# The order of units around the last attention pair, and the leftover tile of a mixture layer

## The chip, the cores and the metric

The kernel runs on one core of a Trainium2 chip. Its engines have their own instruction queues and meet through semaphores: PE (matrix products), DVE (vector), ACT (activations and copies), POOL (casts, and DMAs that convert types or use indices) and SP (which here only issues DMAs). The metric is the device time of one execution in microseconds (us), as the median over runs. Lower is better.

## The reference

Attention with one shared key and value head, then a mixture of 16 experts in 4 groups, one expert per token:

```
scores = scale * np.matmul(q, k.transpose(0, 1, 3, 2))      # q (8, 16, 384, 64), k and v (8, 1, 384, 64)
attn = softmax(scores);  out = np.matmul(attn, v)
x = out as (8 * 384, 16 * 64)                               # 3072 tokens of 1024
g = argmax(x @ w_group)                                     # 4 groups, with weight g_w (softmax)
e = argmax(x @ w_expert[g])                                 # 4 experts of the group, with weight e_w
out[token] = g_w * e_w * (relu(x[token] @ w1[g, e]) @ w2[g, e])
```

In the data that is drawn, nearly all tokens of a batch item choose one expert. The kernel makes use of that, and computes what is left over by itself.

## The kernel before

**Attention.** It works in 24 pairs p of a batch item b (8) and a third st of its 384 tokens. For each pair `scores` (L251) makes six blocks of 64 keys on PE, ACT takes exponentials (L253), DVE sums them over blocks (`pre_add`, L259 and L261) and folds the sum over keys (`fold_keys`, L265). `values` (L290) multiplies the exponentials with v, six blocks into one PSUM tile `o`. `join` (L273) adds the folded sums on PE, `invert` (L278, L280) inverts and spreads them, and `weigh` multiplies `o` by them (L300) to xT, the token rows transposed; POOL casts them to xbf (L301), and after an item's third pair SP writes xbf to DRAM (L303, x_bf). The loop over p runs the scores of pair p beside the values of pair p - 1. The values of the last pair have no scores beside them; they come behind the loop, L611 to L615.

**Gates and weights.** `gates` (L312) makes an item's gate logits on PE, `counts` (L338, L340) counts on PE how many tokens chose each expert, ACT copies the counts from PSUM (L342), and DVE picks the most frequent expert from the first third (`choose_b`). POOL's queue then loads that expert's weights, w1 in four DMAs of 512 KB (L145) and w2 in one of 2 MB (L357), casting f32 to bf16. Weight tiles have two buffers. `gate_c` (L386 to L395) makes each token's weight for the chosen expert, gsel, and marks further pairs of item and expert that any token chose.

**Units.** The chosen expert is computed for the item's 384 tokens in 14 units, which `fill(n)` takes from a list: 8 h units (L407: eight matmuls of 384 columns; ACT ReLU L408 into hT) and 6 y units (L415: eight matmuls of 512 columns; ACT scales them by gsel, L416, into a row tile y, which SP stores when both halves are there, L436). h0 to h7 and y0 to y5 below are an item's units. `fill` follows the 24 pairs in bursts (`PHASES`): the 8 h units of item 6 are the last burst in the loop, after pair 22, with the gates of item 7 after three of them, the counts after five and `early_pair` after six. Its y units come two at a time behind the loop.

**The leftover tile.** `early_pair` (L511) picks the one (item, expert) pair that is expected to be left over, as an index into 128 pairs; `fill` starts loading its w1 after item 6's last h unit and its w2 (L547) after item 6's last y unit. Behind the loop the kernel counts and ranks that pair's tokens: a prefix product on PE (L642, L643, `pr`), a selection matrix of up to 32 tokens, `pick`, in four copies (L653), and their weights and output rows (L659, `pg`; `gc`, `rows`). The item's tokens are read back from x_bf (L626, `xe`), which waits for the write of L303. They are transposed on PE (L681, `pb`), gathered by `pick` (L692, `px`), multiplied by w1 (L700, `ph`), transposed (L705, `phT`) and multiplied by w2 (L712, `py`), with copies on DVE and ACT between. Quarters of the columns lie in four groups of 32 partitions. POOL scatters the result into `out` by rows (L715), which replaces what the y units stored there, and so waits for the earlier stores of `out`. In the kernel before all item 7's units stand ahead of `px`. Then a flag in a register of each engine (`rare`) decides whether a general path runs; with this data it does not.

Order on each engine is as written: PE, DVE, ACT, POOL and SP run their instructions in the order in which the program names them. PSUM tiles named by `side` share three buffers, so each waits until the one three places back was read.

Of the kernel before, what the change touches and what calls it, by code (L numbers as in the profile page):

```python
# [9 lines left out]
FP32 = mybir.dt.float32  # L10
# [3 lines left out]
P = 128  # L14
ACTF = mybir.ActivationFunctionType
# [6 lines left out]
def kernel(  # L22
# [372 lines left out]
        nc.vector.reduce_sum(out=gs[:], in_=gm[:], axis=AX)  # L395
        gsel[b] = gs

    def moe_units(w1, w2, xb, gs_of, place, store):
        units = []
        state = {}  # L400

        def h_unit(fc):
            if fc == 0:
                state["h"] = pool.tile([P, FO, S], BF16, tag="hT", bufs=1, name="hT")
            ps = side([P, CW], FP32, "hps")
            for ko in range(KO):
                nc.tensor.matmul(out=ps[:, 0:S], lhsT=w1[:, ko, fc * P:(fc + 1) * P], rhs=xb[:, ko, :], start=(ko == 0), stop=(ko == KO - 1))  # L407
            nc.scalar.activation(out=state["h"][:, fc, :], in_=ps[:, 0:S], func=ACTF.Relu)  # L408

        def y_unit(st, nh):  # L410
            cs = slice(nh * CW, (nh + 1) * CW)
            y = place(st, cs)
            ps = side([P, CW], FP32, "yps")
            for fo in range(FO):
                nc.tensor.matmul(out=ps[:], lhsT=state["h"][:, fo, st * P:(st + 1) * P], rhs=w2[:, fo, nh * CW:(nh + 1) * CW], start=(fo == 0), stop=(fo == FO - 1))  # L415
            nc.scalar.activation(out=y, in_=ps[:], func=ACTF.Copy, scale=gs_of()[:, st:st + 1])  # L416
            store(st, cs, y)

        for fc in range(FO):
            units.append(lambda fc=fc: h_unit(fc))  # L420
        for st in range(ST):
            for nh in range(2):
                units.append(lambda st=st, nh=nh: y_unit(st, nh))
        return units

    def first_units(b):
        rows = {}

        def place(st, cs):
            if cs.start == 0:  # L430
                rows[st] = pool.tile([P, Dm], FP32, tag="y", bufs=3, name="y")
            return rows[st][:, cs]

        def store(st, cs, y):
            if cs.stop == Dm:
                nc.sync.dma_start(out=outv[b, :, st, :], in_=rows[st][:])  # L436
        return moe_units(wts[b][0], wts[b][1], xbf[b], lambda: gsel[b], place, store)

    NP = B * ST

# [70 lines left out]
    def early_pair():  # L511
        last = B - 1
        mask = pool.tile([P, GE], FP32, tag="mask", bufs=1, name="mask1")
        idf = pool.tile([P, 1], FP32, tag="idf", bufs=1, name="idf1")
        nc.vector.tensor_copy(out=idf[:], in_=choice[last][:, 0:1])
        nc.vector.tensor_scalar(out=mask[:], in0=iota16[:], scalar1=idf[:, 0:1], scalar2=None, op0=OP.is_equal)
        nc.vector.scalar_tensor_tensor(out=extra[:, last * GE:NPAIR], in0=seen[last], scalar=0.0, in1=mask[:], op0=OP.is_gt, op1=OP.subtract)
        known = pool.tile([P, 1], FP32, tag="known", bufs=1, name="known")
        nc.vector.reduce_sum(out=known[:], in_=extra[:], axis=AX)
        top = pool.tile([P, 8], FP32, tag="top", bufs=1, name="top2")  # L520
        idx = pool.tile([P, 8], U32, tag="idx2", bufs=1, name="idx2")
        nc.vector.max_with_indices(out_max=top[:], out_indices=idx[:], in_=extra[:])
        pf = pool.tile([P, 1], FP32, tag="pf", bufs=1, name="pf")
        nc.vector.tensor_copy(out=pf[:], in_=idx[:, 0:1])
        base = pool.tile([P, 1], U32, tag="base", bufs=1, name="base")
        nc.vector.tensor_scalar(out=base[:], in0=idx[:, 0:1], scalar1=NPAIR - GE, scalar2=None, op0=OP.bitwise_and)
        basef = pool.tile([P, 1], FP32, tag="basef", bufs=1, name="basef")
        nc.vector.tensor_scalar(out=basef[:], in0=base[:], scalar1=float(S // GE), scalar2=None, op0=OP.mult)
        gi = pool.tile([P, ST, 2], FP32, tag="gi", bufs=1, name="gi")
        nc.vector.tensor_scalar(out=gi[:, :, 1], in0=tokid[:], scalar1=basef[:, 0:1], scalar2=None, op0=OP.add)  # L530
        reg = nc.values_load(idx[0:1, 0:1], engines=(ET.Pool, ET.DVE, ET.SP), min_val=0, max_val=NPAIR - 1, skip_runtime_bounds_check_because="an index into 128 flags")
        leftover.update(known=known, pf=pf, gi=gi, reg=reg)

    def parts_of(pair):
        e_reg = nc.s_assert_within(pair & (GE - 1), 0, GE - 1, skip_runtime_bounds_check_because="the bits of an index below 128")
# [13 lines left out]
    for p in range(NP):  # L549
# [50 lines left out]
        if p in PHASES:  # L600
            n = PHASES[p]
            steps = {}
            prep_q(p + 1)
            steps = {2: lambda: gates(b), 4: lambda: (counts(b, b - 1), turns(p))}
            if b == B - 1:
                steps[5] = early_pair
            for i in range(n):
                fill(1)
                if i in steps:
                    steps[i]()  # L610
    join(NP - 1)  # L611
    for j in range(KB):
        values(NP - 1, j)
    invert(NP - 1)
    weigh(NP - 1)  # L615
# [21 lines left out]
    nc.vector.tensor_add(out=mb[:, 1, 3:4], in0=mb[:, 1, 2:3], in1=m[:, 2:3])  # L637
    nfl = pool.tile([P, 1], FP32, tag="nfl", bufs=1, name="nfl")
    nc.vector.reduce_sum(out=nfl[:], in_=extra[:], axis=AX)
    fill(2)  # L640
    pr = side([P, CW], FP32, "pr")
    nc.tensor.matmul(out=pr[:, 0:4], lhsT=prefix[:], rhs=mb[:, 0, :], start=True, stop=False)  # L642
    nc.tensor.matmul(out=pr[:, 0:4], lhsT=ones_bf[:], rhs=mb[:, 1, :], start=False, stop=True)  # L643
# [9 lines left out]
        nc.vector.tensor_scalar(out=pick[:, st, :], in0=rank_of[:], scalar1=rk[:, st:st + 1], scalar2=m[:, st:st + 1], op0=OP.is_equal, op1=OP.mult)  # L653
    pick_bf = pool.tile([P, ST, CAP], BF16, tag="kT", name="pick_bf")
    nc.vector.tensor_copy(out=pick_bf[:], in_=pick[:, :, 0:CAP])
    fill(2)
    pg = side([P, CW], FP32, "pg")
    for st in range(ST):
# [4 lines left out]
    rows = pool.tile([P, 1], U32, tag="rows", bufs=1, name="rows")  # L663
    nc.vector.tensor_copy(out=rows[:], in_=gc[:, 1:2])

    nc.vector.tensor_sub(out=small[:, 1:2], in0=nfl[:], in1=small[:, 0:1])
    nex = pool.tile([1, 1], I32, tag="nex", bufs=1, name="nex")
    nc.vector.tensor_copy(out=nex[:], in_=small[0:1, 1:2])
# [3 lines left out]
    nc.vector.tensor_add(out=raref[:, 0:1], in0=raref[:, 0:1], in1=raref[:, 1:2])  # L672
    rarei = pool.tile([1, 1], I32, tag="rarei", bufs=1, name="rarei")
    nc.vector.tensor_copy(out=rarei[:], in_=raref[:, 0:1])
    fill(2)

    xtok = []
    for st in range(ST):
# [4 lines left out]
        nc.vector.tensor_copy(out=xt[:], in_=pb[:])  # L683
        xtok.append(xt)
        fill(1)
    fill(len(units) - 1)
    rare = nc.values_load(rarei[0:1, 0:1], min_val=0, max_val=2, skip_runtime_bounds_check_because="a sum of two comparisons")
    fill(1)
    px = side([P, KO, CAP], FP32, "px")
    for ko in range(KO):  # L690
        for st in range(ST):
# [1 line left out]
    xc = pool.tile([P, KO, CAP], BF16, tag="qT", bufs=3, name="xc")  # L693
    nc.vector.tensor_copy(out=xc[:], in_=px[:])

    w1c, w2c = leftover["w1"], leftover["w2"]
    ph = side([P, QW], FP32, "ph")
    for ko in range(KO):
# [1 line left out]
            nc.tensor.matmul(out=ph[CAP * g:CAP * g + CAP, :], lhsT=xc[:, ko, :], rhs=w1c[:, ko, g * QW:(g + 1) * QW], start=(ko == 0), stop=(ko == KO - 1), tile_position=(0, CAP * g))  # L700
    hg = pool.tile([P, QW], BF16, tag="pt", bufs=9, name="hg")
    nc.scalar.activation(out=hg[:], in_=ph[:], func=ACTF.Relu)
    phT = side([P, 2, P], BF16, "phT")
    for h in range(2):
        nc.tensor.transpose(out=phT[:, h, :], in_=hg[:, h * P:(h + 1) * P], identity=ident_bf[:])  # L705
    hc = pool.tile([P, 2, P], BF16, tag="qT", bufs=3, name="hc")
    nc.vector.tensor_copy(out=hc[:], in_=phT[:])
    py = side([P, QW], FP32, "py")
    for g in range(4):
        for h in range(2):  # L710
# [1 line left out]
                nc.tensor.matmul(out=py[CAP * c:CAP * c + CAP, :], lhsT=hc[:, h, CAP * g:CAP * g + CAP], rhs=w2c[:, 2 * g + h, c * QW:(c + 1) * QW], start=(g == 0 and h == 0), stop=(g == 3 and h == 1), tile_position=(0, CAP * c))  # L712
    yc = pool.tile([P, QW], FP32, tag="pt", bufs=9, name="yc")
    nc.scalar.activation(out=yc[:], in_=py[:], func=ACTF.Copy, scale=gc[:, 0:1])
    nc.gpsimd.indirect_dma_start(out=out4, out_offset=bass.IndirectOffsetOnAxis(ap=rows[:], axis=0), in_=yc[:], in_offset=None, bounds_check=4 * N - 1, oob_is_err=False)  # L715

    def load_pair(pair):
        e_reg, b_reg = parts_of(pair)
# [144 lines left out]
```

## Time and profile before

| | |
|---|---|
| median of 4 runs | 465.18 us (463.63 to 467.52) |
| profiled execution | 467.64 us, its span 466.1 us |
| PE busy | 452.4 us (97%), mean granted clock 0.988 |
| DVE, ACT, POOL busy | 306.3 us (66%), 242.0 us (52%), 60.4 us (13%) |
| scores and values on PE | 142.4 us (L251), 143.8 us (L290) |
| h and y units on PE | 86.9 us (L407), 84.5 us (L415) |
| moved by DMA | 74.57 MB, mean 160 GB/s |

The profile is of one execution. A row names the line of the kernel, the engine, the operation, output and inputs. Idle time is given in front of an instruction, with what ended it. A matmul of f32 takes several instructions. "Granted clock" is the share of PE's full clock that it was allowed in a stretch. A DMA row on SP or POOL is the issue; the landing is given apart.

### The profile page before, as it was taken

How to read it: one execution, taken by the hardware profiler on the slowest of the kernel's cores; microseconds unless marked ns; L12 is line 12 of the kernel's file. 1: busy time of each engine (PE TensorE's matmuls, PEld its weight loads, DVE VectorE, ACT ScalarE, POOL GpSimd, SP SyncE). 2: the span in 40 equal slices, each digit the busy share in tenths (PEclk: the TensorE clock that was granted, in tenths of full speed). 3: DMA queues.
4: the chain of work that ended last, by engine and by line, in shares of the span. 5: the costliest groups of instructions: out<-in, count | busy, mean ns of one | idle time of the engine just before them, and what ended most of it. 6: DMA issues, size and time to landing. Idle time of an engine off the chain costs nothing. (4 is left out here: it accounts for less than half of the span.)

```text
span 466.1 us, 10157 instructions
## 1 busy us (share of the span) xinstructions
PE 452.4 (97%) x4191; PEld 201.5 (43%) x4191; DVE 306.3 (66%) x483; ACT 242.0 (52%) x344; POOL 60.4 (13%) x83
## 2 busy tenths in 40 slices
PE   8999999999999999999999999999999999979992
PEld 7343445333643345333543336433553336324641
DVE  3999965499708985299725997099843997634400
ACT  2967643675347643576336663576345673603331
POOL 1004003000210103000030013000030001400000
PEclk9999999999999999999999999999999999979997
DMA  8786997996599296984899576992969710999971
GB/s 161 90 142 103 216 214 115 260 191 148 95 203 247 55 199 98 257 174 103 137 133 270 96 159 107 225 234 74 170 100 265 142 69 1 171 211 261 261 183 61
DMA packets 152166, 74.57 MB, mean 160 GB/s; under 512 B 120216, under 2 KB 138652, under 8 KB 152112
## 3 DMA queue, kind: packets, MB, share of 16 engines
q0 software_dynamic: 28416, 37.84, 48.0%
q1 hardware_dynamic: 122368, 35.68, 32.8%
q8 instruction: 35, 0.57, 0.5%
q10 hardware_dynamic: 1328, 0.33, 0.4%
q14 instruction: 19, 0.16, 0.1%
HBM read 92.62 MB, written 19.01 MB: 239 GB/s over the span
## 5 line engine op out<-in xcount | busy, mean ns | idle before, releaser
L253 ACT ACTIVATE pt<-s 128x1024 f32<-128x1024 f32 x144 | 142.1, 1026 | 71.8 <-PE s L251 71.1
L290 PE MATMUL o<-pt,v 64*64 64x512 f32 x1152 | 143.8, 601 | 0.0
L251 PE MATMUL s<-qT,kT 64*64 64x512 f32 x1152 | 142.4, 594 | 0.3 <-ACT qT L229 0.2
L261 DVE TENSOR_TENSOR presum<-presum,pt 128x1024 f32<-128x1024 f32 x96 | 116.6, 1215 | 15.2 <-ACT pt L253 9.8
L407 PE MATMUL hps<-xbf,w 128*128 128x384 bf16 x512 | 86.9, 326 | 0.0
L415 PE MATMUL yps<-w,hT 128*128 128x512 bf16 x384 | 84.5, 379 | 0.5 <-ACT y L416 0.5
L259 DVE TENSOR_TENSOR presum<-pt 128x1024 f32<-128x1024 f32 x24 | 29.4, 1224 | 75.7 <-ACT pt L253 74.2
L290 PEld LDWEIGHTS o<-pt,v 64*64 64x64 f32 x1152 | 44.4, 136 | 78.9 <-issue 74.9
L251 PEld LDWEIGHTS s<-qT,kT 64*64 64x64 f32 x1152 | 40.8, 133 | 66.9 <-issue 60.0
L416 ACT ACTIVATE y<-yps,gsel 128x512 f32<-128x512 f32 x48 | 33.0, 687 | 64.3 <-PE yps L415 60.7
L407 PEld LDWEIGHTS <-w 128*128 128x128 bf16 x512 | 48.2, 98 | 37.3 <-issue 6.5
L301 POOL CAST xbf<-xT 128x1024 bf16<-128x1024 f32 x24 | 25.0, 1041 | 302.7 <-DVE xT L300 302.7
L408 ACT ACTIVATE hT<-hps 128x384 bf16<-128x384 f32 x64 | 31.3, 489 | 51.6 <-PE hps L407 49.0
L415 PEld LDWEIGHTS <-hT 128*128 128x128 bf16 x384 | 37.3, 98 | 45.4 <-issue 1.5
L300 DVE TENSOR_TENSOR xT<-o,rinv 128x1024 f32<-128x1024 f32 x24 | 29.2, 1216 | 7.1 <-PE o L290 7.1
L145 POOL DMA_DIRECT2D w<-in_moe_w_dram x36 | 24.8, 707 | 59.9 <-DVE gsel L395 52.5
L280 DVE STREAM_TRANSPOSE rinv<-rc 128x1024 f32<-128x1024 f32 x24 | 29.9, 1245 | 0.8
L265 DVE TRANSPOSE_TENSOR_REDUCE fold<-presum 128x32 f32<-128x1024 f32 x24 | 29.6, 1232 | 0.0
L243 DVE STREAM_TRANSPOSE qT<-qraw 128x1024 f32<-128x1024 f32 x20 | 23.6, 1202 | 0.0
L209 ACT ACTIVATE qraw<-qraw 128x1024 f32<-128x1024 f32 x21 | 22.0, 1048 | 0.0
L273 PEld LDWEIGHTS sm<-fold,sel 64*64 64x64 f32 x192 | 7.4, 136 | 16.6 <-issue 16.6
L318 DVE STREAM_TRANSPOSE L<-gps 128x32 f32<-128x32 f32 (+1 forms) x16 | 3.7, 229 | 13.6 <-PE gps L312 13.6
(143 smaller groups left out, 158.4 us busy)
## 6 DMA issues: line engine op xcount, KB each, us to landing
w<-in_moe_w_dram POOLq DMA_DIRECT2D x36, 512.0 KB, 11.5
w<-in_moe_w_dram POOLq DMA_DIRECT2D x9, 2048.0 KB, 26.0
out_dram<-y SPq DMA_DIRECT2D x24, 512.0 KB, 6.8
qraw<-in_q_dram SPq DMA_DIRECT2D x56, 192.0 KB, 3.5
x_bf<-xbf SPq DMA_DIRECT2D x8, 768.0 KB, 4.0
v<-in_v_dram SPq DMA_DIRECT2D x16, 96.0 KB, 3.1
k<-in_k_dram SPq DMA_DIRECT2D x28, 48.0 KB, 2.6
qn<-in_q_dram SPq DMA_DIRECT2D x4, 256.0 KB, 4.6
```

What stands on the lines that cost most here:

```text
L251: nc.tensor.matmul(out=ps[64 * c:64 * c + 64, a, :], lhsT=kT[b][r, j * D:(j + 1) * D], rhs=qT[p][r, c * CW:(c + 1) * CW], start=True, stop ...
L253: nc.scalar.activation(out=t[:], in_=ps[:], func=ACTF.Exp, scale=scale)
L259: nc.vector.tensor_add(out=presum[p][:], in0=pt[p, 0][:], in1=pt[p, 1][:])
L261: nc.vector.tensor_add(out=presum[p][:], in0=presum[p][:], in1=pt[p, j][:])
L265: nc.vector.tensor_reduce(out=fold[p][:], in_=presum[p][:].rearrange("p a (n i) -> p (a n) i", i=32), axis=AX, op=OP.add, apply_transpose= ...
L280: nc.vector.transpose(out=t[:].rearrange("p (b i) -> p b i", i=32), in_=rc[:].rearrange("p c b -> p (c b)").unsqueeze(2).to_broadcast([P, ...
L290: nc.tensor.matmul(out=o_ps[p][64 * a:64 * a + 64, c, :], lhsT=v_sb[b][r, j, :], rhs=pt[p, j][r, a, :], start=(j == 0), stop=(j == KB - 1))
L300: nc.vector.tensor_mul(out=xT[b][:, :, ts], in0=o_ps[p][:].rearrange("p c (h n) -> p (c h) n", n=P), in1=rinv[p][:].rearrange("p (h n) -> ...
L407: nc.tensor.matmul(out=ps[:, 0:S], lhsT=w1[:, ko, fc * P:(fc + 1) * P], rhs=xb[:, ko, :], start=(ko == 0), stop=(ko == KO - 1))
L408: nc.scalar.activation(out=state["h"][:, fc, :], in_=ps[:, 0:S], func=ACTF.Relu)
L415: nc.tensor.matmul(out=ps[:], lhsT=state["h"][:, fo, st * P:(st + 1) * P], rhs=w2[:, fo, nh * CW:(nh + 1) * CW], start=(fo == 0), stop=(fo ...
L416: nc.scalar.activation(out=y, in_=ps[:], func=ACTF.Copy, scale=gs_of()[:, st:st + 1])
```

## The change

- Behind the loop three y units of item 6 run ahead of the last pair's values, and `join` of the last pair comes behind two of its six blocks of values.
- In the burst after pair 22, item 7's gates come after two h units (before: three), the counts of its first third after three, and the counts of item 6 with `early_pair` after four (before: both counts after five, `early_pair` after six).
- Behind the last pair, one unit instead of two stands between the counts and `pr`, and one instead of two between `pg` and the first `pb`. Item 7's y units stand between the steps of the leftover tile: one after `px` and its copy, one after `ph`, one after `phT`, one after `py`, one after `spread` and the scatter, and the last behind the flag's load.
- The scatter leaves out the last 128 rows of `out`. If the leftover pair is of item 7, its rows in that block are added there: `final` says so, `of_last` is the selection of the last 128 tokens, transposed on PE; `spread` multiplies it with the leftover tile's result in four matmuls on PE, and two ACT copies bring that to SBUF. For the last row block DVE scales the y unit's PSUM and adds (in place of ACT's scaling), the last unit runs as two of 256 columns, and each part is stored by itself.

```diff
-    def moe_units(w1, w2, xb, gs_of, place, store):
+    def moe_units(w1, w2, xb, gs_of, place, store, merge=None, parts=lambda st, nh: 1):
...
         def y_unit(st, nh):
-            cs = slice(nh * CW, (nh + 1) * CW)
-            y = place(st, cs)
-            ps = side([P, CW], FP32, "yps")
-            for fo in range(FO):
-                nc.tensor.matmul(out=ps[:], lhsT=state["h"][:, fo, st * P:(st + 1) * P], rhs=w2[:, fo, nh * CW:(nh + 1) * CW], start=(fo == 0), stop=(fo == FO - 1))
-            nc.scalar.activation(out=y, in_=ps[:], func=ACTF.Copy, scale=gs_of()[:, st:st + 1])
-            store(st, cs, y)
+            for i in range(parts(st, nh)):
+                n = CW // parts(st, nh)
+                cs = slice(nh * CW + i * n, nh * CW + (i + 1) * n)
+                y = place(st, cs)
+                ps = side([P, n], FP32, "yps")
+                for fo in range(FO):
+                    nc.tensor.matmul(out=ps[:], lhsT=state["h"][:, fo, st * P:(st + 1) * P], rhs=w2[:, fo, cs], start=(fo == 0), stop=(fo == FO - 1))
+                if merge is None or not merge(st, cs, ps, y):
+                    nc.scalar.activation(out=y, in_=ps[:], func=ACTF.Copy, scale=gs_of()[:, st:st + 1])
+                store(st, cs, y)
...
         def store(st, cs, y):
-            if cs.stop == Dm:
+            if closes(st):
+                nc.sync.dma_start(out=outv[b, :, st, cs], in_=y)
+            elif cs.stop == Dm:
                 nc.sync.dma_start(out=outv[b, :, st, :], in_=rows[st][:])
+
+        def closes(st):
+            return b == B - 1 and st == ST - 1
+
+        def merge(st, cs, ps, y):
+            if not closes(st):
+                return False
+            nc.vector.scalar_tensor_tensor(out=y, in0=ps[:], scalar=gsel[b][:, st:st + 1], in1=leftover["y"][:, cs], op0=OP.mult, op1=OP.add)
+            return True
+        return moe_units(wts[b][0], wts[b][1], xbf[b], lambda: gsel[b], place, store, merge, lambda st, nh: 2 if closes(st) and nh == 1 else 1)
+
+    def spread():
+        lo = [ps_m.tile([P, 2, CW], FP32, tag="o", name="lo"), side([P, 2, CW], FP32, "lo2")]
+        for i in range(2):
+            for c in (i, 2 + i):
+                r = slice(CAP * c, CAP * c + CAP)
+                nc.tensor.matmul(out=lo[c // 2][:, c % 2, 0:QW], lhsT=leftover["spread"][r, :], rhs=leftover["yc"][r, :], start=True, stop=True, tile_position=(CAP * c, 0))
+        t = pool.tile([P, Dm], FP32, tag="pt", bufs=9, name="yl")
+        for i in range(2):
+            nc.scalar.copy(out=t[:, i * CW:(i + 1) * CW].rearrange("p (c n) -> p c n", c=2), in_=lo[i][:, :, 0:QW])
+        leftover["y"] = t
...
+        final = pool.tile([P, 1], FP32, tag="final", bufs=1, name="final")
+        nc.vector.tensor_scalar(out=final[:], in0=base[:], scalar1=float(NPAIR - GE), scalar2=None, op0=OP.is_equal)
...
-            steps = {2: lambda: gates(b), 4: lambda: (counts(b, b - 1), turns(p))}
             if b == B - 1:
-                steps[5] = early_pair
+                steps = {1: lambda: gates(b), 2: lambda: counts(b, None), 3: lambda: (counts(None, b - 1), early_pair())}
+            else:
+                steps = {2: lambda: gates(b), 4: lambda: (counts(b, b - 1), turns(p))}
...
-    join(NP - 1)
+    fill(3)
     for j in range(KB):
+        if j == 2:
+            join(NP - 1)
         values(NP - 1, j)
...
-    fill(2)
+    fill(1)
     pr = side([P, CW], FP32, "pr")
...
+    of_last = pool.tile([P, 2, P], FP32, tag="presum", bufs=1, name="of_last")
+    nc.vector.tensor_scalar(out=of_last[:, 0, :], in0=pick[:, ST - 1, :], scalar1=leftover["final"][:, 0:1], scalar2=None, op0=OP.mult)
     fill(2)
     pg = side([P, CW], FP32, "pg")
...
+    nc.tensor.transpose(out=pg[:, P:2 * P], in_=of_last[:, 0, :], identity=ident[:])
+    nc.vector.tensor_copy(out=of_last[:, 1, :], in_=pg[:, P:2 * P])
+    leftover["spread"] = of_last[:, 1, :]
...
-    fill(2)
+    fill(1)
 
     xtok = []
...
-    fill(len(units) - 1)
-    rare = nc.values_load(rarei[0:1, 0:1], min_val=0, max_val=2, skip_runtime_bounds_check_because="a sum of two comparisons")
-    fill(1)
     px = side([P, KO, CAP], FP32, "px")
...
     nc.vector.tensor_copy(out=xc[:], in_=px[:])
+    fill(1)
...
     nc.scalar.activation(out=hg[:], in_=ph[:], func=ACTF.Relu)
+    fill(1)
...
     nc.vector.tensor_copy(out=hc[:], in_=phT[:])
+    fill(1)
...
     nc.scalar.activation(out=yc[:], in_=py[:], func=ACTF.Copy, scale=gc[:, 0:1])
-    nc.gpsimd.indirect_dma_start(out=out4, out_offset=bass.IndirectOffsetOnAxis(ap=rows[:], axis=0), in_=yc[:], in_offset=None, bounds_check=4 * N - 1, oob_is_err=False)
+    leftover["yc"] = yc
+    fill(1)
+    spread()
+    nc.gpsimd.indirect_dma_start(out=out4[0:4 * (N - P)], out_offset=bass.IndirectOffsetOnAxis(ap=rows[:], axis=0), in_=yc[:], in_offset=None, bounds_check=4 * (N - P) - 1, oob_is_err=False)
+    fill(1)
+    rare = nc.values_load(rarei[0:1, 0:1], min_val=0, max_val=2, skip_runtime_bounds_check_because="a sum of two comparisons")
+    fill(1)
```

## The prediction

> **What bounds the kernel now.** I read the page's slices first, for where the PE row falls below full and where the granted clock does.
>
> ```profile
> PE   8999999999999999999999999999999999979992
> PEclk9999999999999999999999999999999999979997
> ```
>
> PE is full everywhere but in the slice from 407.9 us and in the last one; only there can a change of order gain much. Next the timeline of 405 to 467 us (start, duration, engine, line; idle time and its releaser in brackets), cut to what carries the sum:
>
> ```profile
> 405.11 2.75 PE L290 MATMUL o<-pt,v 64*64 64x512 f32 x24
> ...
> 410.95 0.41 PE L273 MATMUL sm<-fold,sel 64*64 64x16 f32 x8 [3.09 <-DVE fold L265]
> ...
> 411.16 8.23 PE L290 MATMUL o<-pt,v 64*64 64x512 f32 x48
> ...
> 419.50 1.23 DVE L300 TENSOR_TENSOR xT<-o,rinv 128x1024 f32<-128x1024 f32 x1 [6.45 <-PE o L290]
> ...
> 428.16 0.19 ACT L342 COPY cnt<-cps 128x48 f32<-128x48 f32 x1
> ...
> 437.59 0.61 PE L681 MATMUL pb<-ident_bf,xe 128*128 128x128 bf16 x8
> ...
> 459.96 1.09 POOL L715 DMA_INDIRECT out_dram<-yc,rows  x1 [26.32 <-POOLq L767]
> ```
>
> PE stood 3.09 us before the last pair's key sums (L273), and then 48 value matmuls took 8.23 us, where 24 of the same took 2.75 just before. The windows (length, PE busy, ..., granted clock, DMA share, GB/s) say why:
>
> ```profile
> 407.86:410.95 3.09, 0.00 (x1) 0.03 (x1) 2.95 (x3) 0.00 (x0) 1.04 (x1) 0.86 1.16 211
> 411.10:417.00 5.90, 5.90 (x36) 2.01 (x39) 1.60 (x2) 0.00 (x0) 0.00 (x0) 0.51 1.12 212
> 417.00:419.20 2.20, 2.20 (x24) 0.63 (x16) 0.00 (x0) 0.00 (x0) 0.00 (x0) 1.00 1.14 204
> 454.60:458.00 3.40, 2.01 (x63) 1.44 (x62) 0.72 (x2) 1.07 (x2) 0.00 (x0) 1.00 0.39 153
> ```
>
> The clock fell inside the wait: (1 - 0.86) x 2 x 3.09 = 0.87 us of it were at half, so it fell near 410.1, 2.2 us after PE stopped, and came back at about 417.0. In 454.6 to 458.0 PE stood 1.4 us in pieces and kept its clock. Last the DMA issues, with the us to landing:
>
> ```profile
> x_bf<-xbf SPq DMA_DIRECT2D x1, 768.0 KB, 7.8
> xe<-x_bf SPq DMA_DIRECT2D x1, 768.0 KB, 7.1
> w<-in_moe_w_dram POOLq DMA_DIRECT2D x1, 2048.0 KB, 16.7
> ```
>
> The leftover tile's rows go out with x_bf (issued 421.86) and come back with xe (issued 429.82), landing at 436.9. Its second weights (issued 432.75) land at 449.5, last of a POOL queue that is never empty from 395.5 on: L145's eight pieces land from 401.4 to 437.1, and L357's block, issued at 398.19 with 22.0 us to landing, at 420.2.
>
> **The change, part by part.** Costs of a unit, start to start: a y unit (8 matmuls of L415) 1.73 us (428.31 to 431.76 holds two), an h unit (L407) 1.30 (435.00 to 437.59 holds two), one key block of values 0.86 (2.75 for three, less the drain).
>
> 1. *Three units before the last values, the join behind two blocks.* fold ends at 410.80. Three y units from 407.8 end at 413.0, two blocks at 414.7, so the join waits for nothing: -3.09. Their weights and hidden rows belong to item 6 and have long been there; their evictions find ACT idle (it did nothing from 407.5 to 421.2). Without the wait the clock stays, so six blocks take 5.15 instead of 8.15 (411.16 to 419.31): -3.0. If the cover were gone, both would be back. The row store of y1 joins SP at about 412, ahead of x_bf, and is issued at once.
>
> 2. *What this does not move.* The last pair's xT now stands behind three more units: 419.31 - 3.09 - 3.0 + 5.2 = 418.4, only 0.9 us earlier. Cast, x_bf and xe hang on it: xe lands at 436.0. On SP xe is now queued behind a row store that waits for y5, evicted at about 425.4; x_bf lands at 428.8, so that is free. With other traffic the pair of transfers could take from 8 us (x_bf's median is 4.0 over the run) to 17 (8.0 each, as the row store issued at 423.7 took); I keep 7.8 and 7.1, since the same queue runs beside it.
>
> 3. *A new wait at pr.* Between the counts (L340) and pr (L642) there were two y units, 3.45 us; now one h unit. The counts come at 418.4 + two y 3.45 + gates 1.04 + y 1.73 + h 1.30 = 425.9. ACT copies them after that unit's ReLU, at 426.55 to 426.75. From that copy's end DVE needed 2.85 us (428.38 to 431.23) to pr's operand, so pr runs at 429.7. The h unit ends at 427.9: PE stands 1.8 us, and behind pr on PE are all remaining h units, whose ReLUs ACT waits for. If ACT copied first, 0.4 less.
>
> 4. *xe takes the place.* pr, two h units, pg 0.6, one h unit: 434.25. The transpose of the closing selection (one f32 128x128 on PE; L228's eight took 1.17) adds 0.15 to 0.3: 434.5. Its two DVE passes (0.33 each by L653's three in 0.98) lie under h units. Then pb needs xe: 436.0, a wait of 1.5. So pb starts at 436.15 instead of 437.59, whatever was gained before; without step 3 the wait would be 3.3.
>
> 5. *After pb.* From 437.59 to the end of L712 at 459.04 were 21.45 us. One h unit less (1.30); the waits between px, ph, phT and py (0.52, 0.49, 0.38) are filled by y units of 1.73, each longer than the eviction it covers (L694 0.42, L702 0.38, L707 0.29), and so are three drains of about 0.2. Added: four f32 matmuls of 256 columns, 0.43 if their four row groups run side by side as the 64*64 tiles of L290 do, 1.7 one after another; I take 0.5, as the rows nearest to it overlap. Halving the last unit adds 0.1. Together 21.45 - 1.30 - 1.39 - 0.6 + 0.6 = 18.8 (to 20.1): PE ends at about 455.1. The closing rows' two ACT copies (0.69 each, as L416) end before y4 and the first half need them; the flag's register load on DVE (0.33) lies between.
>
> 6. *The first choice and its weights.* Gates come one h unit sooner, counts two; DVE's gate arithmetic stands between, so the five weight DMAs start 1.3 to 2.6 us sooner, I take 1.6. The leftover's four behind them still wait for item 6's last h unit, but the queue is full then. Its last block is issued at about 425 instead of 432.75 (after y5) and lands at 449.5 - 1.6 = 447.9. py needs it 12.1 us after pb (three pb 1.35, three h 3.9, px 0.76, three y 5.2, ph and phT 0.9): 448.3. Slack 0.4; unmoved, it would cost 1.2. This also caps the gain: with xe early, py would only wait here.
>
> 7. *The end.* From 459.04 to 466.1 passed 7.06: ACT 0.5, 0.4 to L715, 3.3 to its landing at 463.26, 2.84 to close. Now the scatter waits for row block 1's store: y3 ends 4.2 before PE does, at 450.9; ACT 0.8, store 3.0 (issued at 451.95 before), 0.4, scatter 3.3, close 2.84: 461.3. The last half tile: DVE 0.45, store 2.6 to 3.3, landed at 458.2 to 458.9, level with the scatter's 458.4. POOL's flag load (0.31) now follows the scatter, inside its flight; PE's taken branch (3.48) ends before the close as well. The end is 461.3 to 461.7.
>
> Sum: 466.1 - 461.5 = 4.6 us of the profiled execution (467.64 with 1.5 around its span), which was 2.5 above the median of four. Off the median: 465.2 - 4.6 = 460.6.
>
> **A rule against it.** Steps 3 and 4 leave PE idle for 1.8 and 1.5 us. By the rows, 1.4 us in a window of 3.4 left the clock alone and 2.2 took it; 1.8 lies between, nearer to 2.2 in one piece, so I keep a case for it. The Trainium skill's TensorE: Matmul & The Clock Gate, Part 1, has the clock drop after an idle window of about 3.4 us, free-running; a wait of 3.09 has dropped it here. By that rule alone both new waits would leave the clock whole and the sum stand at 460.6.
>
> **Rivals.** *The clock falls once in the wait at pr.* The row's low stretch lasted 6.9 us (410.1 to 417.0). From 429.8, 4.75 us of work would reach pb at 438.0 instead of 436.0, +2.0; after the second wait nothing absorbs it, +3.4. Against it: both waits are shorter than 2.2. 462.6 to 464.0.
>
> *The transfers come later.* The row stores of y1 and y3 now stand before and right behind x_bf; at 8.0 each, x_bf and xe take 1.1 more, and the last weights, if not 1.6 sooner, 1.2 beyond py. 461.7 to 463.
>
> *The transfers come sooner.* xe at 434.5 and the last weights no later than 446.6 remove the wait of step 4: 459.1; with ACT's copy first 458.7.
>
> *Slower: the clock stays low from pr on.* Each low us costs half a us of work; 3.2 are paid by pb, and 4.6 are paid if it stays low until about 442. Twice the row's 6.9 us, to 443.5, would give about 466; to the first y unit, 469. For it: the second wait comes before a busy stretch as long as the one that brought the clock back (411.1 to 417). Against: one wait alone gave 6.9.
>
> **How the numbers follow.** Forecast 0.60 (459.4 to 462), sooner 0.10, later transfers 0.10, one clock drop 0.14, low clock 0.06. The time is the forecast's, 460.6. 458.6 to 464.2 leaves out the low clock and the rim of the others. 1% is 4.65 us, what runs spread from 463.6 to 467.5 can tell: below 460.5 lie half of the forecast and the sooner case, 0.40; above 469.8 a part of the low clock, 0.03; between them 0.57.
>
> **What would show it.** No wait before L273 and a clock of 1.00 from 408 to 427; PE idle 1.8 us before pr and 1.5 before the first pb; the last weights landing at 447 to 449; no PE gap at ph, phT and py; the scatter 0.4 us behind row block 1's landing. I am wrong if the clock falls after pr, if PE stands at py, or if PE's end and the scatter's landing are more than 4 us apart.

## The result, and the profile after

| | before | after |
|---|---|---|
| median | 464.57 us (78 runs, 463.11 to 467.76) | 463.57 us (52 runs, 462.8 to 464.72) |
| ratio of after to before, 95% interval | | 0.9973 [0.9965, 0.9981] |
| profiled execution, its span | 467.64, 466.1 us | 464.05, 462.5 us |
| mean granted clock of that execution | 0.988 | 0.997 |

The change gains 1.0 us by the medians, 0.27%, where 4.6 were forecast. The two profiled executions differ by 3.6 us, and much of that is not the change: before's stood 3.1 us above its median, after's 0.5.

The slices of after, to be read against those of before:

```profile
PE   8999999999999999999999999999999999999793
PEclk9999999999999999999999999999999999999998
```

The dip of PE in the 36th slice is gone, and a new, shallower one stands in the third from the end. The timeline (start, duration, engine, line; idle time and its releaser in brackets) shows where:

```profile
406.94 5.35 PE L417 MATMUL yps<-w,hT 128*128 128x512 bf16 x24
...
413.99 0.25 PE L273 MATMUL sm<-fold,sel 64*64 64x16 f32 x8
...
414.08 3.64 PE L290 MATMUL o<-pt,v 64*64 64x512 f32 x32
...
417.85 1.23 DVE L300 TENSOR_TENSOR xT<-o,rinv 128x1024 f32<-128x1024 f32 x1 [1.89 <-PE o L290]
...
425.93 0.19 ACT L342 COPY cnt<-cps 128x48 f32<-128x48 f32 x1
...
428.75 0.18 PE L672 MATMUL pr<-mb,prefix 128*128 128x4 bf16 x1 [1.20 <-DVE mb L664]
...
432.78 0.33 PE L698 MATMUL pg<-ident,of_last 128*128 128x128 f32 x1 [0.38 <-DVE gc L694]
...
435.59 0.62 PE L717 MATMUL pb<-ident_bf,xe 128*128 128x128 bf16 x8 [1.18 <-DMA xe<-x_bf]
...
447.92 1.06 PE L749 MATMUL py<-w,hc 128*32 128x256 bf16 x32
...
450.74 0.71 PE L458 MATMUL lo<-yc,of_last 32*128 32x256 f32 x8
...
455.32 1.09 POOL L755 DMA_INDIRECT out_dram<-yc,rows  x1 [29.46 <-DVE y L449]
```

L273 has no wait, and the 32 value matmuls behind it took 3.64 us, full speed. Two waits are new, 1.20 us at `pr` and 1.18 at the first `pb`. This execution began the burst after pair 22 0.85 us sooner than before's (384.24 against 385.09; the code up to there is the same), so 0.85 is added below to compare its times with the forecast's. The windows (length, PE busy, ..., granted clock, DMA share, GB/s):

```profile
407.00:411.00 4.00, 4.00 (x21) 1.81 (x20) 2.95 (x3) 1.08 (x2) 1.04 (x1) 1.00 1.12 211
411.00:418.00 7.00, 7.00 (x64) 2.46 (x63) 1.76 (x3) 0.98 (x2) 0.00 (x0) 1.00 1.10 232
...
428.00:431.00 3.00, 2.12 (x14) 1.31 (x15) 2.69 (x17) 0.49 (x2) 0.00 (x0) 1.00 1.12 300
431.00:435.00 4.00, 3.04 (x21) 1.95 (x18) 1.66 (x12) 1.06 (x3) 0.00 (x0) 1.00 1.12 307
```

The clock is 1.00 throughout, across the two new waits as well (from 435 to 447 it is 1.00 too). Last the DMA issues from 384 us on, with the us to landing at the end:

```profile
x_bf<-xbf SPq DMA_DIRECT2D x1, 768.0 KB, 8.0
xe<-x_bf SPq DMA_DIRECT2D x1, 768.0 KB, 7.2
...
out_dram<-y SPq DMA_DIRECT2D x2, 128.0 KB, 3.5
out_dram<-yc,rows POOLq DMA_INDIRECT x1, 4.3
```

The scatter takes 4.3 us beside the last half tiles' stores; in before, alone at the end, it took 3.3.

### The profile page after: what moved, and what is told of

Its sections match the earlier page's. It is cut to its first block, busy times and chain, and to the rows that moved or that the text cites. A ratio compares the mean times of both kernels' runs of the same rounds, so it can differ in the third digit from the quotient of the medians.

```text
span 462.5 us, 10202 instructions
## 1 busy us (share of the span) xinstructions
PE 450.1 (97%) x4208; PEld 200.5 (43%) x4208; DVE 308.8 (67%) x489; ACT 241.8 (52%) x345; POOL 60.4 (13%) x83
## 5 line engine op out<-in xcount | busy, mean ns | idle before, releaser
L290 PE MATMUL o<-pt,v 64*64 64x512 f32 x1152 | 141.1, 590 | 0.0
L261 DVE TENSOR_TENSOR presum<-presum,pt 128x1024 f32<-128x1024 f32 x96 | 116.6, 1215 | 15.2 <-ACT pt L253 9.8
L417 PE MATMUL yps<-w,hT 128*128 128x512 bf16 (+1 forms) x392 | 85.2, 375 | 0.0
L290 PEld LDWEIGHTS o<-pt,v 64*64 64x64 f32 x1152 | 43.4, 133 | 76.8 <-issue 73.0
L419 ACT ACTIVATE y<-yps,gsel 128x512 f32<-128x512 f32 x46 | 31.6, 687 | 56.9 <-PE yps L417 55.3
L273 PEld LDWEIGHTS sm<-fold,sel 64*64 64x64 f32 x192 | 7.3, 133 | 13.3 <-issue 13.3
L312 PE MATMUL gps<-xT,gw 128*32 128x96 f32 (+2 forms) x576 | 12.6, 239 | 0.0
```

The costliest lines, as they stand in the source:

```text
L261: nc.vector.tensor_add(out=presum[p][:], in0=presum[p][:], in1=pt[p, j][:])
L290: nc.tensor.matmul(out=o_ps[p][64 * a:64 * a + 64, c, :], lhsT=v_sb[b][r, j, :], rhs=pt[p, j][r, a, :], start=(j == 0), stop=(j == KB - 1))
```

## The experiments

Two theories stood at the start. **P**: the low clock behind the join's wait, 3.0 of the forecast's 4.6 us, is met by only a part of before's executions, since it hangs on where the wait falls in the clock's own windows; the profiled execution was one that paid most. **Its rival**: every execution pays it, and the change gives the gain back elsewhere. Later came **X**: what the join gives is spent at the waits for `pr` and `xe`, because the units used as cover ahead of the values are missing there. A median stands with the range of its runs; ratios are to before, run beside it on the same chip (medians there 464.65, 465.54 and 464.88 us in the three groups of runs). None of the three groups lists a run of after, and before's executions without a low clock have medians of 464.19, 464.18 and 464.00 us in them: a difference to after (463.57) of a few tenths of a us is not clear of that.

**1. Before again.** No edit.

> The kernel before, unchanged, to see each execution's granted clock beside its time. Theory P (phase): the clock falls during the wait before the last pair's key sums in only a part of the executions; then the times spread with the clock: executions near 463.5 to 464.5 us have a mean clock of about 0.995, those near 467 us about 0.988, and a fall of 0.007 goes with 3 us. Theory G (given back): the clock falls in every execution, all have a mean clock of about 0.988, and the spread of 463 to 468 us has another cause.

464.45 us (463.68 to 467.29), ratio 0.9994 [0.9973, 1.0015]. Its profiled execution met the same wait and paid less for it. Timeline, then windows:

```profile
409.97 0.30 PE L273 MATMUL sm<-fold,sel 64*64 64x16 f32 x8 [3.09 <-DVE fold L265]
...
410.07 7.09 PE L290 MATMUL o<-pt,v 64*64 64x512 f32 x48
```

```profile
406.80:410.00 3.20, 0.11 (x8) 0.07 (x5) 3.02 (x3) 0.00 (x0) 1.04 (x1) 1.00 1.18 213
410.00:413.50 3.50, 3.50 (x28) 1.44 (x32) 1.60 (x2) 0.00 (x0) 0.00 (x0) 0.62 1.11 210
413.50:417.00 3.50, 3.50 (x32) 1.23 (x24) 0.00 (x0) 0.00 (x0) 0.00 (x0) 0.89 1.13 214
```

The same 3.09 us of wait, but the 48 value matmuls took 7.09 us instead of 8.23. From the windows the low time is (1 - 0.62) x 2 x 3.5 = 2.7 us plus (1 - 0.89) x 2 x 3.5 = 0.8, together 3.4; in the execution behind the forecast it was 6.8, twice as long. The mean clock listed with each execution of before sorts 91 of them:

| mean granted clock | executions | median |
|---|---|---|
| 0.993 and above | 35 | 464.21 us |
| 0.990 to 0.992 | 43 | 465.43 us (+1.2) |
| 0.989 and below | 13 | 467.29 us (+3.1) |

The before_again execution (0.991, 464.92 us) and the one behind the forecast (0.988, 467.64 us) belong to the second and third row. The first row is, by P, a kernel with the wait and without the low stretch. The mean clock also counts PE's idle end, where a low clock costs nothing; in the execution behind the forecast:

```profile
461.50:466.00 4.50, 0.00 (x0) 0.00 (x0) 0.00 (x0) 0.00 (x0) 0.00 (x0) 0.50 0.09 28
```

With the 6.8 us of the wait these 4.5 us at half take (6.8 + 4.5) / 2 / 466 = 0.012 off the mean, which gives the 0.988 listed. So the mean clock alone does not tell a costly stretch from a free one; the rows stand because they hardly overlap in time (463.15 to 464.72, 464.79 to 466.04, 466.00 to 468.04). The next run tests P by taking the idle time alone.

**2. PE kept busy in the wait** (before; the product is not read):

```diff
+    idle = side([P, CW], FP32, "idle")
+    for _ in range(16):
+        nc.tensor.matmul(out=idle[:, 0:S], lhsT=ones_bf[:], rhs=xbf[B - 2][:, 0, :], start=True, stop=True)
     join(NP - 1)
```

> The kernel before with 16 matmuls of 384 columns, whose result nobody reads, on PE ahead of the last pair's key sums: 2.6 us of work inside the wait of 3.1 us, nothing else moved. Theory P (the fall of the clock in that wait hits a part of the executions, 16 of 38 seen so far, by 1.2 or 3.2 us): with PE busy no execution has a mean clock under 0.992, none is over 465.3 us, and the median is that of the executions without a fall, 463.9 to 464.4 us, so at most 0.6 us below before. Theory G (every execution pays 3 us): 461.3 to 462 us.

464.2 us (463.59 to 464.82), ratio 0.9964 [0.9949, 0.998]. Timeline:

```profile
406.84 2.77 PE L613 MATMUL idle<-xbf,ones_bf 128*128 128x384 bf16 x16
409.99 0.30 PE L273 MATMUL sm<-fold,sel 64*64 64x16 f32 x8 [0.38 <-DVE fold L265]
410.10 5.39 PE L290 MATMUL o<-pt,v 64*64 64x512 f32 x48
```

The join comes no sooner, yet the values run at full speed, and the median is that of the first row of the table (464.21), with a spread of 1.2 us in place of some 4. So the low clock comes from the idle time. One execution of the 12 has a mean clock of 0.991, which the expectation had excluded; at 464.82 us it stands only 0.6 above the median, and it has no trace. A median execution of before pays little for the low clock in the 78 runs of the result, 464.57 - 464.21 = 0.36 us, as 43 of them lie at or below 464.72, the top of the first row. In the 91 executions of the table it pays more, 465.19 - 464.21 = 0.98: the share differs between groups of runs.

**3. The join's part alone** (before):

```diff
-    join(NP - 1)
+    fill(3)
     for j in range(KB):
+        if j == 2:
+            join(NP - 1)
         values(NP - 1, j)
```

> The kernel before with one part of the change: three units ahead of the last values, and the join behind two blocks. The leftover tile stays behind all units. P: against the median of before it gains the wait of 3.1 us and a part of the 3.0 us of low clock, and pays about 0.9 us of a wait at pr and 0.6 us at the first pb: 462.0 to 463.2 us, so it is as fast as the whole change or up to 1.5 us faster. G: the whole 6.1 us are gained and about 1.5 paid: 459.5 to 460.5 us, and the whole change must then lose 3 us in its other parts.

461.4 us (460.4 to 461.94), ratio 0.9914 [0.9884, 0.9944]: 2.2 us better than the whole change. It lies below the range of P (462.0 to 463.2) and above that of its rival (459.5 to 460.5): P had expected waits of 0.9 and 0.6 us at `pr` and `pb`, and they did not come. Timeline:

```profile
428.99 0.18 PE L644 MATMUL pr<-mb,prefix 128*128 128x4 bf16 x1
...
435.34 0.62 PE L683 MATMUL pb<-ident_bf,xe 128*128 128x128 bf16 x8
...
451.84 1.06 PE L714 MATMUL py<-w,hc 128*32 128x256 bf16 x32 [0.38 <-DVEq L769]
```

`pr` and `pb` run at the times at which they run in after (428.75 and 435.59), with no wait ahead of them: two more units have been done by then. So the rest of the change costs about 2 us, which gave X.

**4. One unit in place of three** (before):

```diff
-    join(NP - 1)
+    fill(1)
     for j in range(KB):
+        if j == 2:
+            join(NP - 1)
         values(NP - 1, j)
```

> The kernel before with one unit and two blocks of values ahead of the join; the leftover tile stays behind all units. Theory X (units are scarce: each one ahead of the last values is one less that covers the waits at pr and at the first pb, and the last pair's rows come later): beside the three-unit version (461.4 us) the waits of 0.3 to 0.6 us at pr and pb go: 460.7 to 461.3 us. If those waits were absorbed elsewhere: 461.4 us.

461.09 us (460.71 to 461.51), ratio 0.9900 [0.9881, 0.9918]: the lowest median of all kernels here (run 3's range overlaps), 3.1 us under before's executions without a low clock, the whole wait of 3.09. Timeline:

```profile
406.90 1.90 PE L415 MATMUL yps<-w,hT 128*128 128x512 bf16 x8
408.81 1.95 PE L290 MATMUL o<-pt,v 64*64 64x512 f32 x16
410.58 0.25 PE L273 MATMUL sm<-fold,sel 64*64 64x16 f32 x8
```

One y unit and two blocks of values cover the fold. The last pair's tokens then come two units sooner.

**5. The join's part undone** (after):

```diff
-    fill(3)
+    join(NP - 1)
     for j in range(KB):
-        if j == 2:
-            join(NP - 1)
         values(NP - 1, j)
...
-    fill(2)
+    fill(5)
```

> The changed kernel with that one part undone: join and values come first, all five of those units behind them. The last pair's token rows are then ready 2.2 us earlier than in the changed kernel, so nothing waits for their way through DRAM. P: 1 us slower than the changed kernel where the clock does not fall in the wait, 4 us slower where it does: executions spread from 464.5 to 468 us, median 464.5 to 466. G: all executions near 467.5 us.

467.47 us (466.17 to 469.56), ratio 1.0049 [1.0023, 1.0075], 3.9 above after. Its five executions at a clock of 0.994 and above lie at 466.17 to 467.12, the five at 0.991 to 0.992 up to 468.64, the two at 0.989 at 469.5: the spread of P, where the rival had all executions near 467.5. The median lies above what P had expected (464.5 to 466), because the two new waits did not go. Timeline:

```profile
433.23 0.18 PE L670 MATMUL pr<-mb,prefix 128*128 128x4 bf16 x1 [1.20 <-DVE mb L662]
...
440.07 0.62 PE L715 MATMUL pb<-ident_bf,xe 128*128 128x128 bf16 x8 [1.18 <-DMA xe<-x_bf]
```

They are there with the same lengths. The one at `pr` follows the number of units between the counts and `pr`, not the join. The one for `xe` has another cause here: x_bf, issued at 419.49, had landed at 426.1, but on SP `xe` stands behind the row store of y5 and is issued only at 430.02, and it took 10.0 us to land, against 6.7 to 7.2 in all other traces. The prediction's step 2 had named this order on SP and called it free. That the two waits for `xe` are equal is chance; why the transfer took 10.0 is open.

**6. One unit more ahead of `pr`, taken from behind it** (after):

```diff
-    fill(1)
+    fill(2)
     pr = side([P, CW], FP32, "pr")
...
-    fill(2)
+    fill(1)
     pg = side([P, CW], FP32, "pg")
```

> The changed kernel with one h unit moved from behind pr to ahead of it; the number of units ahead of the first pb is the same. The wait at pr (1.2 us, with its second half 1.6) falls to 0.3 us. If the first pb waits for the rows' way through DRAM, as the prediction's fourth step said, that wait takes over what is gained: 463.2 to 463.8 us. If it does not: 462.0 to 462.6 us.

463.42 us (463.07 to 465.76), ratio 0.998 [0.996, 0.9999], no gain on after (463.57). Timeline:

```profile
435.15 0.62 PE L717 MATMUL pb<-ident_bf,xe 128*128 128x128 bf16 x8 [1.67 <-DMA xe<-x_bf]
```

The wait at `pr` is gone and the one for `xe` is 1.67 in place of 1.18. Counted from the burst's start (384.45) `pb` runs 50.70 us later; with the wait at `pr` it does so after 50.52 to 51.35 (runs 9 to 11 and after). So `pb` follows `xe`, whose landing itself varies by 0.8. Two of the 12 executions, at 465.30 and 465.76 us, have a mean clock of 0.991, where none of after's is below 0.994: the longer wait may have lowered the clock in them. The trace is of an execution at 0.998 and cannot show it.

**7. One unit more ahead of each** (after), two fewer between the leftover tile's steps:

```diff
-    fill(1)
+    fill(2)
     pr = side([P, CW], FP32, "pr")
...
-    fill(1)
+    fill(2)
...
-    fill(1)
     w1c, w2c = leftover["w1"], leftover["w2"]
...
-    fill(1)
     py = side([P, QW], FP32, "py")
```

> The changed kernel with one unit more ahead of pr and one more ahead of the first pb, as in the kernel before; two units fewer stand between the leftover tile's steps (none after px, none after phT). Theory X: units are worth more ahead of pr and pb, where 2.8 us were waited, than between the leftover's steps, where the waits were 0.5 and 0.4 us: 461.6 to 462.4 us. Rival: the waits at pr and pb cost nothing, since the last weights or the end set the time: 463.4 to 464.2 us.

462.38 us (461.85 to 462.71), ratio 0.9939 [0.9921, 0.9956], 1.2 better than after. Timeline:

```profile
435.65 0.61 PE L717 MATMUL pb<-ident_bf,xe 128*128 128x128 bf16 x8
...
443.02 1.06 PE L734 MATMUL ph<-w,xc 128*32 128x256 bf16 x32 [0.52 <-DVE xc L728]
...
446.40 1.06 PE L747 MATMUL py<-w,hc 128*32 128x256 bf16 x32 [0.38 <-DVE hc L742]
```

The waits of 1.20 and 1.18 are gone, 0.52 and 0.38 come back at `ph` and `py`, which before had too: 1.5 net in this trace, 1.2 in the medians. X holds for this share.

**8. One unit ahead of the values, one more ahead of `pr` and of the first `pb`** (after):

```diff
-    fill(3)
+    fill(1)
     for j in range(KB):
...
-    fill(1)
+    fill(2)
     pr = side([P, CW], FP32, "pr")
...
-    fill(1)
+    fill(2)
 
```

> The changed kernel with one unit instead of three ahead of the last values; the two others go ahead of pr and ahead of the first pb, one each, as in the kernel before. One unit and two blocks of values (3.4 us) still cover the wait of 3.1 us. Theory X: what the change gives back is that the last pair's token rows are late (three units stand ahead of them) and with them pr and the first pb; then the rows are 3.4 us earlier, the wait at pr falls to about 0.4 us and that at pb to 0, and the last weights (landing near 446.8 us) become the next to be waited for, 1.6 us at py: 1.5 to 2.2 us faster than the changed kernel, 461.2 to 462.2 us. If the two waits did not matter, no more than 0.3 us faster.

462.25 us (461.27 to 463.04), ratio 0.9936 [0.9914, 0.9957], 1.3 better than after. Timeline:

```profile
432.77 0.61 PE L717 MATMUL pb<-ident_bf,xe 128*128 128x128 bf16 x8
...
445.78 1.06 PE L749 MATMUL py<-w,hc 128*32 128x256 bf16 x32 [0.62 <-DMA w<-in_moe_w_dram]
```

`pb` runs 2.8 us sooner than in after, `py` only 2.1: here the last weights are late, the cap of step 6 of the prediction.

**9. The choice at its old step** (after):

```diff
-                steps = {1: lambda: gates(b), 2: lambda: counts(b, None), 3: lambda: (counts(None, b - 1), early_pair())}
+                steps = {2: lambda: gates(b), 4: lambda: counts(b, b - 1), 5: early_pair}
```

> The changed kernel with the gates, counts and the choice of the leftover pair back at their old places after pair 22. The weight DMAs then start about 1.7 us later. If the last weights are not waited for in the changed kernel (they landed at 446.0, py ran at 447.9): no difference, 463.3 to 463.9 us. If the earlier choice is what pays for the leftover tile among the units: 464 to 465.5 us.

463.99 us (463.59 to 464.49), ratio 0.9974 [0.9957, 0.9991], 0.4 above after, between the two expectations and hardly clear of the differences between groups. Timeline:

```profile
448.25 1.06 PE L749 MATMUL py<-w,hc 128*32 128x256 bf16 x32 [0.57 <-DMA w<-in_moe_w_dram]
```

`py` waits for the last weights, which land at 448.2; in after they do at 445.9 (issued 424.97, 20.9 to landing). Counted from the burst's start (384.8 here, 384.24 there) that is 1.8 us later. The wait is real, but `py` itself runs no later than in after, 63.49 us behind the burst's start against 63.68, since in this trace `xe` was waited for 0.35 us and not 1.18. So the earlier choice removes this wait; that it is worth the 0.4 is argued from the medians alone.

**10. Without the closing rows on PE** (after; `of_last` and its transpose go as well):

```diff
         def closes(st):
-            return b == B - 1 and st == ST - 1
+            return False
...
-    spread()
-    nc.gpsimd.indirect_dma_start(out=out4[0:4 * (N - P)], ...)
     fill(1)
...
     fill(1)
+    nc.gpsimd.indirect_dma_start(out=out4, ...)
```

> The changed kernel without its last part: no closing rows on PE, no halves of the last unit; the scatter covers all rows again and stands behind the last unit. Its result is the same. PE ends 1.1 us earlier, but the scatter now waits for the last row block's store: ACT 0.8, store 3.3, 0.9, scatter 3.3, close 2.9 behind PE's end. 2 to 3.3 us slower than the changed kernel, 465.6 to 466.9 us. If the end were set by something else than the scatter, less than 1 us either way.

466.97 us (466.18 to 467.7), ratio 1.0024 [1.0011, 1.0038], 3.4 above after. Timeline:

```profile
460.27 1.09 POOL L752 DMA_INDIRECT out_dram<-yc,rows  x1 [33.94 <-POOLq L804]
```

Counted from the burst's start (384.7) the scatter begins 4.5 us later than in after, as it waits for the last row's store. With the leftover tile between the units, the closing rows' part is worth these 3.4 us.

**11. A scatter that need not wait for item 7's stores** (after): bounded to the first seven items. It leaves out the leftover rows in item 7's first two row blocks.

```diff
-    nc.gpsimd.indirect_dma_start(out=out4[0:4 * (N - P)], ..., bounds_check=4 * (N - P) - 1, oob_is_err=False)
+    nc.gpsimd.indirect_dma_start(out=out4[0:4 * (N - S)], ..., bounds_check=4 * (N - S) - 1, oob_is_err=False)
```

> The changed kernel with the scatter bounded to the first seven items, so that it need not wait for a store of the last item; leftover rows in the last item's first two row blocks would be left out. If the scatter's landing sets the end of the changed kernel (it landed at 459.6, 3 us before the end): the scatter lands near 454.5, the last half's store near 459, PE's jump ends at 459.5: 0.5 to 2 us faster than the changed kernel, 461.5 to 463.1 us. If the last store and the jump set it: within 0.3 us of it.

462.99 us (462.29 to 463.6), ratio 0.9936 [0.9916, 0.9955], 0.6 better than after. Timeline:

```profile
449.89 1.09 POOL L755 DMA_INDIRECT out_dram<-yc,rows  x1 [23.34 <-ACT yc L751]
```

The scatter starts 5.4 us sooner and the end moves by 0.6 only, with six runs whose range overlaps after's. In this trace the last half tile's store lands at about 459.6 (issued at 456.0, 3.6 us), and PE's taken branch behind the flag (from 455.5, 4.15 us) ends at about 459.6 too; which of them sets the end was not separated. In after the scatter lands at 459.6, the last store and the branch at 459.4: three paths end together, and freeing one gives little.

**12. `px` ahead of the last unit** (run 4's kernel):

```diff
-    fill(1)
     px = side([P, KO, CAP], FP32, "px")
...
     nc.vector.tensor_copy(out=xc[:], in_=px[:])
+    fill(1)
```

> The version with one unit ahead of the join, and the leftover tile behind the units but for its gather px, which goes ahead of the last unit, so that the unit covers the copy after px (0.5 us). The scatter then waits 2.2 us for the rest of the chain and not for the last store. 460.4 to 460.8 us, against 461.1 without; if the last store becomes what the scatter waits for, 461.1 or more.

461.82 us (460.79 to 463.54), ratio 0.9934 [0.9911, 0.9957]: 0.7 worse than run 4, where I expected a gain unless the last store became what the scatter waits for. Timeline:

```profile
451.82 0.47 ACT L716 ACTIVATE yc<-py,gc 128x256 f32<-128x256 f32 x1 [1.83 <-PE py L714]
454.56 1.09 POOL L717 DMA_INDIRECT out_dram<-yc,rows  x1 [27.62 <-POOLq L769]
```

The result is there sooner, but the scatter starts 2.3 us behind it where run 4 needed 0.3: the last row's store took 4.0 us in this profile, against 2.7 in run 4 and 3.3 in before, and the scatter waits for it. Why it took longer was not tried.

## Why the prediction was wrong

The direction and nearly every place were right; the gain was 3.6 us too large. The measured time lies in the range, but the forecast's sum does not hold.

**Step 1, the wait: right.** L273 waits for nothing, and runs 3 and 4 show the 3.09 us as real: 2.8 and 3.1 below before's executions without a low clock.

**Step 1, the clock: the step that failed.** "So six blocks take 5.15 instead of 8.15: -3.0" is right for the execution that was profiled and wrong for the median. Only 13 of 91 executions pay that much, 43 pay 1.2 and 35 nothing, and before's median carries 0.36. The forecast then took the whole sum "off the median", although the sentence ahead of that said that the profiled execution stood 2.5 us above it. By the table that distance is this term. Without it the forecast would have been 1.6 us, or 2.0 with the 0.36. This is 2.6 of the 3.6 that it missed, for the 78 runs of the result; with the share of the 91 it would be 2.0.

**Steps 2 to 4: right.** With the 0.85 us, y3 of item 6 starts at 418.50 (forecast for xT 418.4), `xe` lands at 436.4 (436.0), `pr` runs at 429.6 (429.7), the waits are 1.20 and 1.18 (1.8 and 1.5), and `pb` starts at 436.44 (436.15). Run 6 shows step 4's claim that `xe` takes the place of a wait removed at `pr`. The clock rivals did not come: all of after's executions have a mean clock of 0.994 or more.

**Step 5: 0.6 us short.** From `pb` to PE's end passed 19.44 us, forecast 18.8. The spread took 0.64 (450.74 to 451.38; forecast 0.5). The six y units took 10.86 between the leftover tile's products, against 10.36 in one piece in before, where 0.1 more was forecast. Ahead of `pb`, in step 4, the transpose took 0.55, of which 0.38 is a wait for DVE's `gc` (forecast 0.15 to 0.3).

**Step 6: right in kind.** The last weights landed at 446.7 (with the 0.85 us) instead of 447.9, so `py` had 2 us of slack instead of 0.4. In run 9, without the earlier choice, it waited 0.57 (forecast 1.2). Run 8 shows that the weights cap what an earlier `xe` can give.

**Step 7: the second term mis-sized.** The scatter does wait for row block 1's store. With the 0.85 us, that store is issued 0.6 later than forecast, because of PE, and lands after 2.6 us (forecast 3.0); the scatter starts 1.2 us behind the landing (451.56 + 2.6 = 454.16 to 455.32; forecast 0.4) and flies 4.3 us (forecast 3.3). It lands at 460.5 instead of 458.4, and the span closes at 463.35 instead of 461.5. PE's end and the scatter's landing are 4.6 us apart (455.03 and 459.6), beyond the 4 that the prediction gave as a sign of being wrong. The forecast's 0.4 was the distance from ACT's copy to the scatter in before (459.56 to 459.96); the last store had landed there at 458.7 (455.41 + 3.3), 1.2 ahead of the scatter. Of the 1.85 us 0.5 are this execution's place above its median, and 0.35 that before's execution stood above the median of its own row in the table; about 1.0 is left, the other part of the miss. This split rests on one execution of each kernel. Freed of its wait, in run 11, the scatter gave 0.6 by the medians.

**The rivals.** None of the four came. The pair of transfers took 15.2 us (forecast 14.9), so they were neither clearly later nor sooner, and the clock did not fall behind the new waits.

**Where the gain went.** The join's part gives 3.2 us by itself (run 3), and the rest of the change takes 2.2 of them back. Counted from the burst's start, PE ends 2.4 us later in after (455.03, burst at 384.24) than in run 3 (452.90, burst at 384.5). The waits at `pr` and for `xe` add 2.4, spread and transpose 1.2, and the three waits between `px` and `py` that are now filled give 1.4 back: 2.2. The first of these sums is of one trace; the wait for `xe` at the same place was 0.35, 0.57 and 1.22 in runs 9, 11 and 10. Runs 7 and 8 show that the waits can be had back in part by moving units, 1.2 and 1.3 us. Each added part is worth something within the interleaving (runs 9 and 10: 0.4 and 3.4), but the interleaved order as a whole is dearer here than the one that it replaced: with one unit ahead of the join in both, run 8 stands 1.2 us above run 4.

**The rule.** The trace of before had a wait of 3.09 us lower the clock; by mean clock and time it did so in 56 of 91 executions. The two traces show 3.4 and 6.8 us of low clock, and the table's two slower rows are read as one such stretch and two. The Trainium skill's TensorE: Matmul & The Clock Gate, Part 1, has free-running windows of about 3.4 us, and a drop after at least one idle window. The lengths and the differences from execution to execution agree with free-running windows; but a wait of 3.09 us does not fill a window of 3.4 and lowered the clock all the same, so on what it takes to drop this rule and the runs differ, and the measurement decides.

What stays open is the length that it takes. Two waits of 1.2 us lowered the clock in none of after's executions, 3.09 did in part, and run 6, with 1.67, has two executions of 12 that look like it.

## What to carry to other kernels

Before a stretch at low clock is priced, compare the profiled execution's time and mean clock with those of the other runs, and leave PE's idle end out of the clock: a cost that one execution pays belongs to the sum only in the share in which executions pay it. A unit that fills a wait is taken from somewhere: count what it covered there, and use no more than the wait needs (here one unit did what three were spent on). Where a chain of transfers hangs on an event, every unit put ahead of that event delays the chain.

## What was not expected of the hardware

- The same program with the same 3.09 us of idle PE ran its next 48 value matmuls in 8.23 or 7.09 us by the execution, and in 35 of 91 executions mean clock and time show no such stretch. The share changes from one group of runs to another: 14 of 26, 2 of 23 and 11 of 30 executions without it, and 8 of 12 in run 1.
- The scatter starts 1.2 us behind the landing of the store that it waits for: 454.16 to 455.32 in after, 454.48 to 455.64 in run 9, 453.3 to 454.56 in run 12. Where ACT's copy comes last it starts 0.3 to 0.4 us behind that (runs 4 and 11).
- The same scatter's landing took 2.2 to 4.4 us. Behind all stores it took 2.9 to 4.0 in before and in runs 1 to 4 and 12, but 2.4 in run 10; beside the last stores 3.6 to 4.4 (after and runs 5 to 9); ahead of them 2.2 (run 11). What sets it was not tried.
